# Attention beside an MLP on one core: the attention loop by two query blocks, with one stretch of 64x64 tiles for both

## Chip, cores and metric

One core of a Trainium2 chip. The metric is the device time of one execution in microseconds, lower is better.

## The reference

```python
xn = layernorm(x)                                   # x: 2048 x 640
q, k, v = split(xn @ wqkv)                          # 32 heads of 20 columns
scores = (q @ k.T) * 20 ** -0.5
mask = (i - j >= 0) & (i - j < 256)                 # each query sees 256 keys at most
s = softmax(where(mask, scores, -1e9)) @ v          # then @ wo
h = relu(xn @ w1 + b1) ** 2                         # 640 -> 1536
g = silu(h @ w2 + b2)                               # 1536 -> 640
return x + (s @ wo) * g
```

Everything is float32. The kernel splits each float32 operand of a product into two float16 parts, high and low, and adds three products (high by high, high by low, low by high).

## The kernel before

Three parts follow one another. The first normalizes x, turns it, and makes the values and the first 128 query and key columns. The second is the attention loop. The third multiplies the attention's output with `wo` and joins both branches.

The attention loop has 16 head pairs `p` of 16 query blocks `q` of 128 rows, so 256 steps `s`, and 13 more in which the later stages of the last blocks finish. All engines' orders are written out by hand: each engine does its instructions in the order in which the code gives them. In a step, in this order:

- `scores` (L547): for both heads, two half blocks of 64 queries against 320 keys, four products in tiles of 64x64 of the array (L557). `maxima` (L560): VectorE adds the mask and takes the largest score of each row (L568), one instruction a head. Every fourth step `max_rows` (L577) turns the maxima of four blocks on TensorE; they are written by DMA as two more rows of the queries.
- `scores_t` (L596), ten steps behind (`LAG`): the scores once more with keys as rows, the maxima being subtracted by the two more rows, again four 64x64 products (L604). `exps` (L607): ScalarE's exponential of both heads, 768 columns, into `p32` (L609), and two selects on GpSimd that cut the mask's triangles (L610, L612).
- `low` (L620), two steps behind that: VectorE's float16 rest `pl` of the exponentials (L623).
- A part of the filler (`EARLY_FILL`), then `flush`, which empties finished filler groups; then `high` (L615), one step behind `exps`: ScalarE's float16 copy `ph` (L617). Then the rest of the filler.
- `values` (L626), for two blocks in every second step: products of `ph` and `pl` with the values (L637), 24 for two blocks. Every fourth block `normed` (L641) copies the sums (L644), and VectorE and GpSimd divide.

The filler (`filler`, L804) is a generator of all other products, so that TensorE has work in each step: 32 groups of 15 products of 512 columns for the other query and key columns (`qkps`), then for 8 blocks of 256 rows 12 groups of 15 products of 256 columns (`hps`, the hidden layer) and 4 groups of 36 products of 320 columns (`yps`), and at the end the output product (`wops`, from L922). `fill` (L995) takes from it as much as the step's share `per`. When a group is finished, its evacuation is put on a list: for `qkps` a ScalarE copy and a VectorE rest (L80, L81); for `hps` ScalarE's relu and square (L855, L856), VectorE's square (L858) and a subtraction on GpSimd (L859); for `yps` one VectorE instruction (L886). `tick` (L739) splits one waiting piece of weights into its parts, ScalarE first, then VectorE (L125, L126), or squares it (L775).

The eight PSUM banks of 2 KiB (512 float32 columns) a partition are dealt out in pools: three for filler groups (`pmm`), two for scores (`pat`), two for turned scores (`pst`, one tile `sts[0]`, L594), one for the values' sums (`po_`).

Of the kernel before, what the change touches and what calls it, by code (L numbers as in the profile page):

```python
# [14 lines left out]
P = 128  # L15
# [19 lines left out]
LAG = 10  # L35
PB = 6
# [3 lines left out]
EARLY_FILL = 0.35  # L40
SWING = 0.3
# [16 lines left out]
def attn_mlp_kernel(ctx: ExitStack, tc, x, wqkv, wo, w1, b1, w2, b2, out):  # L58
# [4 lines left out]
    pmm = ctx.enter_context(tc.tile_pool(name="pmm", bufs=3, space=PSUM))  # L63
    pat = ctx.enter_context(tc.tile_pool(name="pat", bufs=2, space=PSUM))
    pst = ctx.enter_context(tc.tile_pool(name="pst", bufs=1, space=PSUM))
    po_ = ctx.enter_context(tc.tile_pool(name="po", bufs=1, space=PSUM))
# [148 lines left out]
    with tc.tile_pool(name="ph1v", bufs=4) as p1v, tc.tile_pool(name="ph1", bufs=2) as p1, tc.tile_pool(name="ph1x", bufs=4) as p1b, tc.tile_pool(name="ph1w", bufs=1) as p1w:  # L215
        xts, xns, mvs, rstds, turns, vts = {}, {}, {}, {}, {}, {}
        wv = [p1w.tile([P, KC, D], F16, name=f"wv{p}") for p in range(2)]
        sums = po_.tile([P, 64], F32, tag="o", name="sums")
# [312 lines left out]

    at1 = ctx.enter_context(tc.tile_pool(name="at1", bufs=1))
# [12 lines left out]
    mts = {}  # L545

    def scores(p, q, between):  # L547
        i = p % 2
        r = [pat.tile([P, 4 * P], F32, tag="s", name="sps") for h in range(2)]
        rows = between and between(r[0])  # L550
        nk = min(WIN + HB, (q + 1) * P)
        for j in range(2):
            q0 = q * P + j * HB
            k0 = max(0, q0 - WIN)
            for h, ps in enumerate(r):
                rows_ = slice(HB * h, HB * h + HR)
                nc.tensor.matmul(ps[HB * j:HB * (j + 1), :nk], qs[i][rows_, q0:q0 + HB], ks[i][rows_, k0:k0 + nk], start=True, stop=True)  # L557
        return (r, mask if q > 1 else mask0[:, 2 * P - nk:], nk), rows

    def maxima(p, q, r):  # L560
        if q % 4 == 0:
            mts[p, q // 4] = mtp_.tile([P, 8], F32, tag="mt", name="mt")
        mt = mts[p, q // 4]
        r, mk, nk = r
        for h, ps in enumerate(r):
            junk = mtp_.tile([P, WIN + HB], BF16, tag="junk", name="junk")
            at_ = 4 * h + q % 4
            nc.vector.tensor_tensor_reduce(out=junk[:, :nk], in0=ps[:, :nk], in1=mk, scale=1.0 / MAX_UNIT, scalar=-3.0e38, op0=ALU.add, op1=ALU.max, accum_out=mt[:, at_:at_ + 1])  # L568
        if q % 4 == 3:
            mp = mps[q // 4 % 2]  # L570
# [6 lines left out]
    def max_rows(p, g, tp=None):  # L577
        i = p % 2
        mp = mts.pop((p, g))
        if tp is None:  # L580
            tp = pat.tile([P, 4 * P], F32, tag="s", name="mtp")
        tp = tp[:, 3 * P:3 * P + P // 2].bitcast(F16)
# [9 lines left out]
    pts = {}  # L592
    ots = {}
    sts = []  # L594

    def scores_t(p, kb):  # L596
        i = p % 2
        n = min(3, NT - kb) * P
        ps = sts[0]
        for j in range(2):  # L600
            c0, c1 = HB * j, min(n, WIN + HB * (j + 1))
            for hh in range(2):
                rows_ = slice(HB * hh, HB * hh + ER)
                nc.tensor.matmul(ps[HB * j:HB * (j + 1), hh, c0:c1], ks[i][rows_, kb * P + HB * j:kb * P + HB * (j + 1)], qs[i][rows_, kb * P + c0:kb * P + c1], start=True, stop=True)  # L604
        return ps, n

    def exps(p, kb, ps, n):  # L607
        p32 = at2.tile([P, 2, 3 * P], F32, tag="p32", bufs=3, name="p32")
        nc.scalar.activation(p32[:, :, :n], ps[:, :, :n], AF.Exp, scale=esc[0], bias=ebias)  # L609
        nc.gpsimd.affine_select(p32[:, :, 0:P], p32[:, :, 0:P], pattern=[[0, 2], [1, P]], compare_op=ALU.is_ge, fill=0.0, base=0, channel_multiplier=-1)  # L610
        if n == 3 * P:
            nc.gpsimd.affine_select(p32[:, :, 2 * P:], p32[:, :, 2 * P:], pattern=[[0, 2], [-1, P]], compare_op=ALU.is_gt, fill=0.0, base=0, channel_multiplier=1)  # L612
        return p32

    def high(p, kb, p32, n):  # L615
        ph = at4.tile([P, 2, 3 * P], F16, tag="ph", name="ph")
        nc.scalar.activation(ph[:, :, :n], p32[:, :, :n], AF.Copy)  # L617
        phs[p, kb] = (ph, p32, n)

    def low(p, kb):  # L620
        ph, p32, n = phs.pop((p, kb))
        pl = at4.tile([P, 2, 3 * P], F16, tag="pl", bufs=PB - 1, name="pl")
        nc.vector.tensor_sub(pl[:, :, :n], p32[:, :, :n], ph[:, :, :n])  # L623
        pts[p, kb] = (ph, pl)

    def values(p, q):  # L626
        if q % 4 == 0:
            ots[p, q // 4] = po_.tile([P, 4, 2, VW], F32, tag="o", name="ops")
        ot = ots[p, q // 4]
        vp = vps[p]  # L630
        ksr = list(range(max(0, q - 2), q + 1))
        for hh in range(2):
            m = 0
            for k in ksr:
                for t in pts[p, k]:
                    m += 1
                    nc.tensor.matmul(ot[:, q % 4, hh, :], t[:, hh, (q - k) * P:(q - k + 1) * P], vp[:, k // 4, k % 4, hh, :], start=m == 1, stop=m == 2 * len(ksr))  # L637
        if q >= 2:
            del pts[p, q - 2]

    def normed(p, g):  # L641
        ot = ots.pop((p, g))
        osb = at2.tile([P, 8, VW], F32, tag="osb", name="osb")
        nc.scalar.activation(osb, ot.rearrange("p a h w -> p (a h) w"), AF.Copy)  # L644

        def rest():
            rs = at2.tile([P, 8], F32, tag="rs", name="rs")
            nc.vector.reciprocal(rs, osb[:, :, VW - 1])
            on = at2.tile([P, 8, DH], F32, tag="on", name="on")
            nc.gpsimd.tensor_add(on, osb[:, :, 0:DH], osb[:, :, DH:2 * DH])  # L650

            def last():
                nc.gpsimd.tensor_mul(on, on, rs.unsqueeze(2).to_broadcast([P, 8, DH]))
                post(o_d[g].rearrange("t p d -> p t d")[:, :, 2 * DH * p:2 * DH * (p + 1)], on.rearrange("p (t h) d -> p t (h d)", t=4))
            norm.append(last)
        return rest


    early = at2.tile([P, 1], F32, tag="early", bufs=1, name="early")
    state = [0.0, 0.0, 0]  # L660
# [10 lines left out]
    pending, late = [], []  # L671
# [5 lines left out]
    def flush(upto=None):  # L677
        for f in late[:]:
            f()
        late.clear()  # L680
        while pending and (upto is None or flushed[0] < upto):
            flushed[0] += 1
            pending.pop(0)()

# [32 lines left out]
    AGE = 2  # L717
# [65 lines left out]
    def second_scales():  # L783
        s2, i2 = weight_scale("w2", totals("w2_t", pmm.tile([P, NF], F32, tag="mm", name="sums2"), mlp["g2"]))
        so, io = weight_scale("wo", totals("wo_t", pmm.tile([P, KC], F32, tag="mm", name="sumso"), sso))
# [18 lines left out]
    def filler():  # L804
        ws = {1: {w: tuple(qkw[0][:, 1, i, j] for j in range(2)) for i, w in enumerate("qk")}}
        for g in range(1, KC):
            ensure(f"g{g}")
            for b in range(NB):
# [17 lines left out]
                for w in "qk":  # L826
                    hi, lo = ws[g][w]
                    ps = pmm.tile([P, BT], F32, tag="mm", name="qkps")
# [271 lines left out]
```

## Time and profile before

| | us |
|---|---|
| median of three runs | 849.09 (848.74 to 850.21) |
| profiled execution | 848.83 |
| its span | 847.0 |
| before the attention loop | 118.7 |
| attention loop | 648.8 |
| output product and end | 79.5 |

The span is the time from the first to the last instruction in the trace. An engine's busy time is the union of its instructions' times. Consecutive instructions of one engine overlap a little, so what an instruction costs its engine is read from its start to the next one's start, where nothing is waited for.

### The profile page before, as it was taken

The page shows a single profiled execution, that of the slowest core. Times are in us where ns is not written, and L with a number is a line of the kernel's source. Part 1 is how long each engine was busy: PE and PEld are TensorE (multiplying, and loading weights), DVE is VectorE, ACT ScalarE, POOL GpSimd, SP SyncE. Part 2 cuts the span into 40 slices and gives each one's busy share as a digit, 9 for nine tenths or more (in the row PEclk, how much of TensorE's full clock was granted, in tenths as well). Part 3 has the DMA queues.
Part 4 walks back from the last instruction along what each step waited for, and adds up shares of the span by engine and source line. Part 5 has one row for each costly group of instructions (what it writes and reads, how often), then busy time and mean ns, then how long its engine had stood idle before and what let it go on. Part 6 is the DMA issues. An engine that isn't in the chain of part 4 may idle for free.

```text
span 847.0 us, 25061 instructions
## 1 busy us (share of the span) xinstructions
PE 822.7 (97%) x9426; PEld 553.4 (65%) x9426; DVE 692.8 (82%) x1897; ACT 648.1 (77%) x1028; POOL 485.0 (57%) x874
## 2 busy tenths in 40 slices
PE   8999998999999999999999999999999999999998
PEld 7765553444444676776766766766767767767775
DVE  6776566788999998898988998888988888975655
ACT  5565446998898997897997997987987988993321
POOL 2000001456665798796896986886986977961000
PEclk9999999999999999999999999999999999999999
DMA  7994349755475311213111222113122113055883
GB/s 245 250 349 129 135 127 283 234 162 157 127 229 163 111 44 55 66 33 89 51 49 50 65 52 65 50 33 84 30 76 65 49 42 99 11 180 171 301 297 126
DMA packets 100498, 104.52 MB, mean 123 GB/s; under 512 B 42520, under 2 KB 72856, under 8 KB 100376
## 3 DMA queue, kind: packets, MB, share of 16 engines
q1 hardware_dynamic: 100376, 102.91, 39.8%
q8 instruction: 74, 1.21, 0.6%
q14 instruction: 48, 0.39, 0.2%
HBM read 65.67 MB, written 36.83 MB: 121 GB/s over the span
## 4 chain that ended last, share of the span: by engine, by line
PE 60%; ACT 14%; POOL 8%; DVE 7%; issue 6%; DMA 3%; SPq 1%; DVEq 0%; ACTq 0%; POOLq 0%
PE yps L882 17%; PE wops L688 8%; PE vps L292 7%; PE hps L688 6%; ACT p L609 5%; PE ops L637 5%; PE qkps L688 5%; PE sps L557 4%; ACT ph L617 3%; PE qkps L503 3%; DVE junk L568 3%; PE stps L604 2%; POOL hh L859 2%; DVE pl L623 2%; ACT relu L855 2%
## 5 line engine op out<-in xcount | busy, mean ns | idle before, releaser
L609 ACT ACTIVATE p<-stps,ebias,esc 128x768 f32<-128x768 f32 (+2 forms) x256 | 242.1, 946 | 59.7 <-PE stps L604 48.9
L568 DVE CUSTOM_DVE_ANT_0 junk<-sps,mask 128x320 bf16<-128x320 f32 (+2 forms) x512 | 220.8, 468 | 49.0 <-PE sps L557 41.4
L623 DVE TENSOR_TENSOR pl<-p,ph 128x768 f16<-128x768 f32 (+2 forms) x256 | 248.8, 972 | 3.8 <-ACT ph L617 3.2
L610 POOL TENSOR_SCALAR_AFFINE_SELECT p<-p 128x256 f32<-128x256 f32 x256 | 163.8, 640 | 86.0 <-ACT p L609 76.7
L617 ACT ACTIVATE ph<-p 128x768 f16<-128x768 f32 (+2 forms) x256 | 203.1, 793 | 2.4 <-POOL p L612 1.6
L688 PE MATMUL hps<-xT,w 128*128 128x256 f16 x1440 | 176.2, 273 | 0.0
L882 PE MATMUL yps<-w,hh 128*128 128x320 f16 x1152 | 174.6, 300 | 0.0
L688 PEld LDWEIGHTS <-w 128*128 128x128 f16 x1440 | 132.6, 98 | 36.0 <-issue 17.2
L882 PEld LDWEIGHTS <-hh 128*128 128x128 f16 x1152 | 104.7, 98 | 57.0 <-issue 18.1
L688 PE MATMUL qkps<-xT,qkw 128*128 128x512 f16 x480 | 115.4, 380 | 0.5 <-DVE w_t L153 0.5
L612 POOL TENSOR_SCALAR_AFFINE_SELECT p<-p 128x256 f32<-128x256 f32 x224 | 103.6, 463 | 0.0
L557 PE MATMUL sps<-ks,qs 60*64 60x320 f16 (+2 forms) x1024 | 87.4, 312 | 6.8 <-DVE mt L568 5.9
L637 PE MATMUL ops<-vp,ph 128*128 128x41 f16 x1440 | 89.8, 181 | 0.0
L637 PE MATMUL ops<-vp,pl 128*128 128x41 f16 x1440 | 89.5, 180 | 0.0
L637 PEld LDWEIGHTS <-ph 128*128 128x128 f16 x1440 | 84.5, 96 | 6.2 <-issue 0.6
L604 PE MATMUL stps<-qs,ks 62*64 62x320 f16 (+4 forms) x1024 | 80.9, 293 | 6.7 <-ACT p L609 6.1
L573 POOL CAST mp<-mt 128x8 f16<-128x8 f32 x64 | 44.6, 698 | 70.0 <-DVE mt L568 69.7
L637 PEld LDWEIGHTS <-pl 128*128 128x128 f16 x1440 | 78.9, 96 | 5.6
L859 POOL TENSOR_TENSOR hh<-sq,hh 128x256 f16<-128x256 f32 x96 | 74.9, 782 | 6.4 <-DVE sq L858 4.3
L688 PEld LDWEIGHTS <-qkw 128*128 128x128 f16 x480 | 41.6, 98 | 55.4 <-issue 11.7
L292 PE MATMUL vps<-wv,xT 128*128 128x320 f16 x480 | 70.3, 303 | 3.2 <-ACT xT L261 1.6
L557 PEld LDWEIGHTS <-qs 60*64 60x64 f16 x1024 | 32.5, 103 | 55.2 <-issue 47.4
(150 smaller groups left out, 1032.4 us busy)
## 6 DMA issues: line engine op xcount, KB each, us to landing
ks<-k_d SPq DMA_DIRECT2D x64, 120.0 KB
qs<-q_d SPq DMA_DIRECT2D x64, 120.0 KB
raw<-in_B_w_dram SPq DMA_DIRECT2D x24, 320.0 KB
v_d<-vt SPq DMA_DIRECT2D x8, 656.0 KB
vp<-v_d SPq DMA_DIRECT2D x16, 328.0 KB
xt<-in_A_x_dram SPq DMA_DIRECT2D x16, 320.0 KB
k_d<-shm SPq DMA_DIRECT2D x20, 256.0 KB
q_d<-shm SPq DMA_DIRECT2D x20, 256.0 KB
```

What stands on the lines that cost most here:

```text
L292: nc.tensor.matmul(ps, xT[b][:, xp, c, t * P:(t + 1) * P], wv[wp][:, c, nh * HALF:(nh + 1) * HALF], start=n == 0, stop=n == 3 * KC - 1)
L557: nc.tensor.matmul(ps[HB * j:HB * (j + 1), :nk], qs[i][rows_, q0:q0 + HB], ks[i][rows_, k0:k0 + nk], start=True, stop=True)
L568: nc.vector.tensor_tensor_reduce(out=junk[:, :nk], in0=ps[:, :nk], in1=mk, scale=1.0 / MAX_UNIT, scalar=-3.0e38, op0=ALU.add, op1=ALU.max, ...
L604: nc.tensor.matmul(ps[HB * j:HB * (j + 1), hh, c0:c1], ks[i][rows_, kb * P + HB * j:kb * P + HB * (j + 1)], qs[i][rows_, kb * P + c0:kb * ...
L609: nc.scalar.activation(p32[:, :, :n], ps[:, :, :n], AF.Exp, scale=esc[0], bias=ebias)
L610: nc.gpsimd.affine_select(p32[:, :, 0:P], p32[:, :, 0:P], pattern=[[0, 2], [1, P]], compare_op=ALU.is_ge, fill=0.0, base=0, channel_multip ...
L612: nc.gpsimd.affine_select(p32[:, :, 2 * P:], p32[:, :, 2 * P:], pattern=[[0, 2], [-1, P]], compare_op=ALU.is_gt, fill=0.0, base=0, channel ...
L617: nc.scalar.activation(ph[:, :, :n], p32[:, :, :n], AF.Copy)
L623: nc.vector.tensor_sub(pl[:, :, :n], p32[:, :, :n], ph[:, :, :n])
L637: nc.tensor.matmul(ot[:, q % 4, hh, :], t[:, hh, (q - k) * P:(q - k + 1) * P], vp[:, k // 4, k % 4, hh, :], start=m == 1, stop=m == 2 * le ...
L688: nc.tensor.matmul(ps, a, b_, start=j == 0, stop=j == n - 1)
L882: nc.tensor.matmul(pss[nh], hs[fc][:, hp, tt * P:(tt + 1) * P], lin1(w2t, (2 * fc + wp) * D + nh * HALF, HALF), start=fc == 0 and j == 0, ...
```

## The change

The loop goes by periods `t` of two query blocks: 128 periods and 8 more (`OUT`). A period has this order:

1. `flush`, which empties all finished filler groups; on every second period the turning of the maxima.
2. `values` for two blocks, eight periods behind, into that one of two accumulators `accs` that the filler isn't using, and `taken`, ScalarE's copy of the sums, every period.
3. `low` for two blocks (1536 columns in one instruction), two periods behind `scores_t`.
4. `scores_t` for two blocks, five periods behind (`LAG`), then `scores` for two blocks: one stretch of 64x64 products. Each head has a tile of three banks, `pairs[h]`: scores of the two blocks in columns 0 to 320 and 320 to 640, the turned maxima from 640, the turned scores from 768 to 1536. A product that would cross a bank's edge is cut in two there (`cuts`).
5. `exps` of head 0, the maxima of head 1 for both blocks, `exps` of head 1, the maxima of head 0. The selects take all four blocks at once.
6. Filler in four parts of 0.3, 0.3, 0.25 and the rest, with `flush`, stores and loads between them. After the first part `high`, one period behind `exps`, in one instruction of 1536 columns.

A filler group asks for its bank when it begins (`bank`): the accumulator that was not last used, or, late in a period and if it is short, the first bank of a score tile. A group isn't begun if less than `GUARD` of the period's share is left; the rest is made up in the next period. In the last part of the kernel the groups go round all eight banks.

The sort that did the last three hidden groups' products last in the first half block's `yps` groups is gone. The PSUM pools of the first part are closed at its end.

```diff
-LAG = 10
-PB = 6
+LAG = 5
+OUT = LAG + 3
+PB = 4
+GUARD = 0.7
+LATE = 2.2
+BANK = 512
...
+    psum = ctx.enter_context(tc.tile_pool(name="psum", bufs=1, space=PSUM))
+    pairs = [psum.tile([P, 3 * BANK], F32, name=f"pair{h}") for h in range(2)]
+    accs = [psum.tile([P, BANK], F32, name=f"acc{i}") for i in range(2)]
...
+    SCORE_AT = (0, WIN + HB)
+    TURNED_AT = 2 * (WIN + HB)
+    TSCORE_AT = 3 * BANK - 6 * P
+
+    def cuts(o, n):
+        x = [o] + [y for y in range(BANK, 3 * BANK, BANK) if o < y < o + n] + [o + n]
+        return list(zip(x, x[1:]))
...
+    def bank(cost, n=BANK):
...
+        if state[0] > state[4] + LATE and cost < state[3] - state[0] - GUARD and used != {2, 3}:
+            key = 2 + len(used)
+            used.add(key)
+        else:
+            last[0] = key = 1 - last[0]
+        flush(owner.get(key, 0))
+        return key, (accs + pairs)[key][:, 0:n]
...
+            if e:
+                ot = accs[1 - last[0]][:, 0:4 * VW].rearrange("p (q h w) -> p q h w", q=2, h=2)
+                values(*e, ot)
+                norm = taken(*e, ot)
+            if c:
+                low(c)
             if b:
-                stp = scores_t(*b)
-            if a:
-                maxima(*a, sc)
...
+                scores_t(*b)
+                p32s[b] = at2.tile([P, 3 * BANK], F32, tag="p32", bufs=3, name="p32")
+            if a:
+                scores(*a)
+            for h in range(2):
+                if b:
+                    exps(b[1], p32s[b], h)
+                if a:
+                    for q in range(2):
+                        maxima(a[0], 2 * a[1] + q, 1 - h)
...
+            fill(0.3 * per)
+            between()
+            tick()
+            d = at(t - LAG - 1)
             if d:
-                low(*d)
...
+                high(d, p32s.pop(d))
+            fill(0.3 * per)
+            between()
+            fill(0.25 * per)
+            between()
             tick()
-            if c:
-                high(*c, *exs.pop(c))
...
+            fill(state[3] - state[1])
```

`between` is `flush`, the stores that are due, and loads.

More of the change, by code (lines that the diff above doesn't have):

```diff
@@ L545, in attn_mlp_kernel @@
     mts = {}
-    def scores(p, q, between):
-        i = p % 2
[L549 to L558, printed above, removed]
@@ L615, in high @@
[L615 to L639, printed above, removed]
@@ L1005, in attn_mlp_kernel, with at, between @@
     with tc.manual_schedule(engines={E_.PE, E_.Activation, E_.DVE, E_.Pool, E_.SP}):
[L1006 to L1012 removed]
+        p32s, loads = {}, []
+        def at(n):
+            return divmod(n, NT // 2) if 0 <= n < count else None
+        def between():
+            flush()
             post_all()
             issue(RATE)
[L1015 removed]
+        for t in range(periods):
+            state[2] = t
+            post_all()
+            issue(RATE)
+            a, b, c, e = (at(t - lag) for lag in (0, LAG, LAG + 2, OUT))
@@ L1034, in attn_mlp_kernel @@
-            rows = between = None
-            if s % 4 == 1 and 1 < s <= NP * NT + 1:
-                def between(tp=None, s=s):
-                    return max_rows((s - 2) // NT, (s - 2) % NT // 4, tp)
-            if a:
-                sc, rows = scores(p, q, between)
-            elif between:
-                rows = between()
+            flush()
+            used.clear()
+            rows = max_rows((t - 2) // (NT // 2), (t - 2) % (NT // 2) // 2) if t % 2 == 0 and 2 <= t <= count else None
```

279 lines of the change are left out of this document (152 added, 127 removed).

## The prediction

> **What bounds the kernel now.** I read the page's busy shares first, then the stretches of the trace in which the filler is of one kind, then single rows of three engines. The shares are TensorE (PE), VectorE (DVE), ScalarE (ACT) and GpSimd (POOL):
>
> ```profile
> span 847.0 us, 25061 instructions
> PE 822.7 (97%) x9426; PEld 553.4 (65%) x9426; DVE 692.8 (82%) x1897; ACT 648.1 (77%) x1028; POOL 485.0 (57%) x874
> 118.70:281.00 162.30, 155.12 (x1573) 73.22 (x1573) 138.40 (x409) 133.71 (x206) 82.54 (x169) 1.00 0.63 191
> 404.00:434.40 30.40, 30.36 (x445) 23.63 (x444) 28.36 (x79) 29.10 (x50) 27.75 (x46) 1.00 0.18 49
> 495.50:525.80 30.30, 30.30 (x410) 20.14 (x408) 25.44 (x79) 24.82 (x34) 22.65 (x42) 1.00 0.24 68
> 767.50:847.00 79.50, 74.83 (x585) 56.37 (x583) 47.01 (x90) 21.85 (x34) 0.99 (x2) 1.00 0.68 233
> ```
>
> The last four lines are stretches: length, then busy us of PE, PEld, DVE, ACT, POOL, the granted clock (1.00 everywhere) and DMA. The loop over query blocks runs from 118.7 to 767.5, 648.8 us for 269 steps, so two steps (one period of the changed loop) take 4.82 us. The first stretch has qk filler, the second hps, the third yps. PE is the bound on average, but beside hps filler ACT is busy 29.10 of 30.40 us and DVE 28.36: there three engines are full at once. After 767.5 there is only the output product.
>
> What PE pays for a stretch of 64x64 tiles, in the rows of PE (start, us, line, form, count):
>
> ```profile
> 504.03 0.33 PE L557 MATMUL sps<-ks,qs 60*64 60x320 f16 x4
> 504.19 0.31 PE L604 MATMUL stps<-qs,ks 62*64 62x320 f16 x4
> 504.43 1.40 PE L882 MATMUL yps<-w,hh 128*128 128x320 f16 x9
> 505.66 0.18 PE L637 MATMUL ops<-vp,ph 128*128 128x41 f16 x1
> ...
> 508.46 0.25 PE L557 MATMUL sps<-ks,qs 60*64 60x128 f16 x4
> 508.54 0.31 PE L604 MATMUL stps<-qs,ks 62*64 62x320 f16 x4
> ```
>
> Four tiles go as one group: 0.16 us for 320 columns (504.03 to 504.19), 0.08 for 128 (508.46 to 508.54). A line through the two is 0.027 us and 0.00042 a column. From the last group to the first yps it is 0.24, so 0.08 more than the group itself. A yps takes 0.137 (nine from 504.43 to 505.66).
>
> **The change, part by part.** I cost PE first, then the order of the other engines.
>
> *One stretch for two blocks.* One way out of the tile mode (0.08 us) goes in each of 128 periods. The way in isn't free of other work in these rows; taken like the way out it makes 0.16 a pair, 20 us in all (at least 10, if the way in costs nothing; at most 26, at 0.2). *Cuts at bank edges:* the second block's scores (columns 320 to 640) become 192 and 128, the first turned block (768 to 1152) becomes 256 and 128. By the line above these are 0.107+0.080 and 0.134+0.080 instead of 0.16 each: 0.08 a period, 10 us (at least 3.5, if only one extra start of 0.027 counts). Net on PE: 20-10, about -10 us, with ends +0 and -22. *Half as many calls:* `high` and `low` handle 1536 columns at once, the two selects four blocks, and the output copy is taken every period. These save or cost about 0.1 us a period on engines beside PE; they enter below by their rows.
>
> *PSUM.* The filler has two accumulators instead of three, and the values take the one that it isn't using. The rule for borrowing a score bank asks that over 2.2 of the 3.125 us of filler be done and that the group be shorter than the rest less 0.7, so under 0.225; the shortest product group is 1.67. It is never used for one inside the loop.
>
> *A new wait.* Each head has one tile of three banks of 512 columns. The second block's scores end at column 640, the turned scores start at 768: both lie in the second bank. ACT's exp reads one, DVE's maxima the other. If two readers of a bank are kept apart, the code's order decides: exp of head 0 beside the maxima of head 1, then exp of head 1 **after** the maxima of head 1. In the kernel before, no bank has two readers that don't already wait for one another by their data, so no row shows this. The nearest row is that exp waits for DVE where they share a tile of SBUF:
>
> ```profile
> ACT p L609 <- PE stps L604: 48.9, 74, 1.8
> ACT p L609 <- DVE pl L623: 7.6, 12, 1.4
> PE stps L604 <- ACT p L609: 6.1, 17, 1.1
> PE sps L557 <- DVE mt L568: 5.9, 7, 1.6
> ```
>
> The columns are total us, times, longest. The last two are what PE waits for the readers now, 12 us at most to be gained. Below zero the new wait can't go; at zero it leaves the PE sum. What it costs at most follows from what stands in front of the maxima on DVE. I take the wait as real: the heads are crossed in the code for that, and an order between users of one tile is what the second row shows.
>
> *The chain that this closes.* DVE's order in a period is `low`, the maxima of head 1 (two), of head 0 (two), then what the filler needs. `low` needs `high` of the period before. `high` stands behind both exps on ACT. So exp of head 1 -> `high` -> `low` of the next period -> two maxima -> exp of head 1: a period can't be shorter than that. The rows:
>
> ```profile
> 407.86 0.99 ACT L609 ACTIVATE p<-stps,ebias,esc 128x768 f32<-128x768 f32 x1 [0.58 <-DVE ysb L886]
> 408.75 0.56 ACT L855 ACTIVATE relu<-hps,m,m 128x256 f32<-128x256 f32 x1
> 409.34 0.42 ACT L856 ACTIVATE hh<-relu 128x256 f16<-128x256 f32 x1
> 409.66 0.83 ACT L617 ACTIVATE ph<-p 128x768 f16<-128x768 f32 x1
> 410.39 0.98 ACT L609 ACTIVATE p<-stps,ebias,esc 128x768 f32<-128x768 f32 x1
> 416.90 0.61 ACT L617 ACTIVATE ph<-p 128x512 f16<-128x512 f32 x1
> 417.42 0.97 ACT L609 ACTIVATE p<-stps,ebias,esc 128x768 f32<-128x768 f32 x1
> ...
> 408.18 0.47 DVE L568 CUSTOM_DVE_ANT_0 junk<-sps,mask 128x320 bf16<-128x320 f32 x1
> 408.59 0.94 DVE L623 TENSOR_TENSOR pl<-p,ph 128x768 f16<-128x768 f32 x1
> 409.46 0.41 DVE L858 TENSOR_TENSOR sq<-relu 128x256 f32<-128x256 f32 x1
> 413.27 1.25 DVE L623 TENSOR_TENSOR pl<-p,ph 128x768 f16<-128x768 f32 x1
> 414.44 0.62 DVE L858 TENSOR_TENSOR sq<-relu 128x256 f32<-128x256 f32 x1
> 418.47 0.68 DVE L623 TENSOR_TENSOR pl<-p,ph 128x512 f16<-128x512 f32 x1
> 419.07 0.68 DVE L858 TENSOR_TENSOR sq<-relu 128x256 f32<-128x256 f32 x1
> ```
>
> Start to start, exp takes 0.89 (407.86 to 408.75). `high` takes 0.73 for 768 columns (409.66 to 410.39) and 0.52 for 512, so 0.21 for 256 more: 1.36 for 1536, and its end is 0.10 later (0.83 against 0.73). `low` takes 0.87 (408.59 to 409.46) and 0.60 for 512, so 1.68 for 1536. A maximum takes 0.41 to the next and 0.47 to its end. From one engine's end to the next's start I take 0.03, the gap after relu's end (408.75+0.56 to 409.34). Sum: 0.89+1.46+0.03+1.68+0.41+0.47+0.03 = 4.97 us. The last two key blocks of a head pair are narrower by half (768 columns for 1536): about 0.1 less on exp, 0.5 on `high`, 0.7 on `low`, and its first maxima are shorter by 0.3: 1.6 in 8 periods, mean 4.77. With it closed on 121 of the 136 periods (it starts at the seventh and ends when the scores do): 577 us. The first 7 and last 8 have less work; by filler (3.1) and a part of the stretch and values I take 25 and 31 us. So far 633, less than 648.8: alone the chain is no loss.
>
> *What stands in the chain.* The code fixes where each filler group is emptied: before `high` (first flush of the period) or behind it. Walking through it, of 96 hps groups 31 come before `high` and 65 behind. Before: relu and square, 409.66-408.75 = 0.91 on ACT, all in the chain. Behind: relu runs after `high`, DVE's sq waits for it, and `low` of the next period waits behind sq. That is 0.56+0.03+0.41, less the 0.13 from `high`'s own end: 0.87. Sum 28+57 = 85 us. For qk groups:
>
> ```profile
> 206.03 0.59 ACT L80 ACTIVATE shm<-qkps 128x512 f16<-128x512 f32 x1
> 206.50 0.84 ACT L617 ACTIVATE ph<-p 128x768 f16<-128x768 f32 x1
> 206.69 0.69 DVE L81 SCALAR_TENSOR_TENSOR shm<-qkps,shm 128x512 f16<-128x512 f32 x1
> ...
> 211.46 0.83 ACT L125 ACTIVATE qkw<-raw,g_s 128x640 f16<-128x640 f32 x1
> 212.18 0.84 ACT L617 ACTIVATE ph<-p 128x768 f16<-128x768 f32 x1
> ```
>
> After the seventh period 9 come before `high` (0.47 each) and 17 behind (0.59+0.03+0.69-0.13 = 1.18): 4+20 = 24 us. The 35 weight pieces (0.72 on ACT each) sit before `high` or after it in turn; 25 of them in the chain make 18 (0 to 50). yps groups are emptied by DVE alone, in the time in which it waits for `high`: nothing. If that cover went, 32 evacuations of a maximum's length (0.47), 15 us.
>
> **The sum.** 633+85+24+18 = 760 us against 648.8: +111. PE's ten us don't count, since its work of some 4.65 us a period (4.82 less 10 us of saving and 12 of waits over 128 periods) fits under the chain. Behind 767.5 the tail keeps its 79.5; eight banks there instead of the present set may give 1. The profiled execution took 848.83 us for its 847.0 span, 0.3 under the median of 849.09. Prediction: 848.8+111 = **960 us**. The ends of this case: 915 if half the emptying terms hide (-64) while `low` is dearer (1.17 for 768 columns from 413.27 to 414.44; half of that excess is 0.15 a period, +18), and 995 if all pieces are in the chain (+32).
>
> The Trainium skill speaks against this change here: "PSUM — Partial Sum Buffer", section "PSUM bank collisions raise a hardware error", says that two engines on one bank and quadrant at once raise an error, two readers included, and that the compiler puts a dependency between them. No run here shows it yet. By it the time is 960; without it, the first rival's 833.
>
> **The rivals.** *No wait between the readers (other side).* ACT and DVE run free, PE stays the bound, and gets its -10 and about 6 of the 12 us of waits: 849-16 = **833** (820 to 845). It decides if exp of head 1 starts at exp of head 0's end while `low` still runs. For it: PE's 97%, and no row of such a wait. Against: both lie in one bank. *The chain holds but the emptying hides.* Its plain 4.77 with half or less of the 127 us of terms: 633+30 to 633+64, and the 200 us outside the loop, so **863 to 897**. For it: DVE idles in yps stretches (25.44 of 30.30). Against: in the hps stretch nothing is idle that could hide it. *Nothing measurable, 849:* no wait between readers, but ACT sets the hps stretches. Its 29.10 us there don't shrink, and two accumulators behind `high` make PE wait what the stretch saves: 51 periods of 0.2 against -10.
>
> **Chances.** The chain as summed 0.70 (its own range 915 to 995); chain with hidden emptying 0.12; no wait 0.13; nothing 0.05. A difference of 0.2% (1.7 us) is about what this kernel's runs can tell. Slower: 0.70+0.12, less 0.02 for the lower edge of the second; faster: 0.13 and a little of the last, 0.14; same 0.06. The range takes the first two cases and the last: 848 to 995, which leaves out the 833 and a tail above, under 0.2.
>
> **What would show it.** In the changed profile: exp waiting for the maxima's line on DVE, around 100 times, in sum over 80 us; `low` of some 1.7 us waiting for `high`; hps stretches near 41 us instead of 30.4 and yps ones near 30; PE's share under 90%; four maxima in a row behind `low`. In PE's rows, one stretch in a period with groups of 0.13, 0.08, 0.16, 0.16, 0.11, 0.08. I am wrong if exp of head 1 follows that of head 0 by 0.9 us in most periods, or if hps stretches stay at 30.

## The result, and the profile after

The changed kernel takes 1032.01 us (1026.98 to 1033.41, four runs), the kernel before 848.91 beside it: ratio 1.214, 95% interval 1.210 to 1.219. It is 183 us slower; 960 was predicted. One of the two executions of the variant exps_first below took 2006 us at full granted clock, for a reason that isn't known, and is left out. The profiled execution of the changed kernel took 1031.83 us. The page's span, busy shares and chain:

```profile
span 1030.1 us, 26382 instructions
PE 841.4 (82%) x10386; PEld 595.8 (58%) x10386; DVE 673.3 (65%) x1786; ACT 665.6 (65%) x1012; POOL 438.9 (43%) x634
ACT 33%; PE 25%; DVE 20%; issue 19%; DMA 2%; SPq 0%; ACTq 0%; POOL 0%; DVEq 0%
```

PE's share fell from 97% to 82%, and no engine took its place: ACT and DVE are less busy than before too. So waits between engines are the first suspect. From the list of waits, without GpSimd's and the weight loads' (us in total, times, longest):

```profile
ACT p L623 <- DVE mt L576: 121.1, 104, 2.8
DVE sq L900 <- ACT relu L897: 104.3, 86, 2.3
DVE pl L645 <- ACT ph L638: 55.1, 47, 1.8
PE acc L658 <- ACT relu L897: 45.3, 45, 2.0
PE acc L658 <- DVE shm L79: 25.7, 17, 3.5
PE acc L728 <- ACT relu L897: 25.5, 21, 3.1
```

The first is the predicted wait: exp (L623) waits for the maxima (L576). In the timeline of the two engines beside hps filler it stands with its whole chain, ACT first, then DVE (start, us; in brackets the idle time before):

```profile
571.68 0.99 ACT L623 ACTIVATE p<-pair,ebias,esc 128x768 f32<-128x768 f32 x1 [1.69 <-DVE mt L576]
572.57 1.47 ACT L638 ACTIVATE ph<-p 128x1536 f16<-128x1536 f32 x1
573.94 0.56 ACT L897 ACTIVATE relu<-acc,m,m 128x256 f32<-128x256 f32 x1
574.85 0.55 ACT L897 ACTIVATE relu<-acc,m,m 128x256 f32<-128x256 f32 x1
576.03 0.99 ACT L623 ACTIVATE p<-pair,ebias,esc 128x768 f32<-128x768 f32 x1
578.71 0.99 ACT L623 ACTIVATE p<-pair,ebias,esc 128x768 f32<-128x768 f32 x1 [1.69 <-DVE mt L576]
...
575.50 0.62 DVE L900 TENSOR_TENSOR sq<-relu 128x256 f32<-128x256 f32 x1 [0.48 <-ACT relu L897]
576.05 1.75 DVE L645 TENSOR_TENSOR pl<-p,ph 128x1536 f16<-128x1536 f32 x1
577.72 0.48 DVE L576 CUSTOM_DVE_ANT_0 junk<-pair,mask 128x320 bf16<-128x320 f32 x1
578.13 0.48 DVE L576 CUSTOM_DVE_ANT_0 junk<-pair,mask 128x320 bf16<-128x320 f32 x1
```

Exp of head 1 at 571.68, `high`, two relus, DVE's sq behind the second, `low`, two maxima, exp of head 1 at 578.71: 7.03 us, with no idle time over 0.1 us between a step and the next (ACT's squares behind the relus are left out of the rows). Beside yps filler, where only the bare chain is left, the same exp starts at:

```profile
608.53 0.99 ACT L623 ACTIVATE p<-pair,ebias,esc 128x768 f32<-128x768 f32 x1 [1.21 <-DVE mt L576]
613.61 0.99 ACT L623 ACTIVATE p<-pair,ebias,esc 128x768 f32<-128x768 f32 x1 [1.62 <-DVE mt L576]
```

That is 5.08 us for a period (predicted 4.97). The stages of qk filler, of one block's hps filler, of one block's yps filler, and the tail, by windows (length, busy us of PE, PEld, DVE, ACT, POOL, granted clock, DMA):

```profile
121.00:327.00 206.00, 160.28 (x1818) 83.86 (x1814) 139.07 (x383) 135.85 (x200) 60.98 (x115) 0.93 0.48 149
480.70:521.80 41.10, 30.56 (x455) 25.36 (x455) 27.38 (x74) 31.40 (x50) 26.38 (x34) 0.96 0.14 38
596.30:628.00 31.70, 28.30 (x422) 20.79 (x421) 22.97 (x66) 22.60 (x28) 20.85 (x26) 1.00 0.20 58
923.00:1030.00 107.00, 82.60 (x553) 56.36 (x550) 46.42 (x88) 22.04 (x32) 0.00 (x0) 0.93 0.49 176
```

Measured from the first qk product to the first output product, the loop takes 801.9 us (before 650.6: +151), what is ahead of it 121.2 (118.9: +2), and the tail behind it 107.1 (77.6: +30). So two places lost the time, the loop and the tail.

### The profile page after: what moved, and what is told of

It reads as the page before. It is cut to its first block, busy times and chain, and to the rows that moved or that the text cites. A ratio compares the mean times of both kernels' runs of the same rounds, so it can differ in the third digit from the quotient of the medians.

```text
span 1030.1 us, 26382 instructions
## 1 busy us (share of the span) xinstructions
PE 841.4 (82%) x10386; PEld 595.8 (58%) x10386; DVE 673.3 (65%) x1786; ACT 665.6 (65%) x1012; POOL 438.9 (43%) x634
## 4 chain that ended last, share of the span: by engine, by line
ACT 33%; PE 25%; DVE 20%; issue 19%; DMA 2%; SPq 0%; ACTq 0%; POOL 0%; DVEq 0%
ACT ph L638 14%; DVE pl L645 10%; ACT p L623 8%; PE acc L728 6%; PE vps L290 6%; PE pair L728 5%; DVE junk L576 5%; ACT relu L897 4%; PE qkps L501 3%; PE acc L658 2%; ACT hh L898 2%; DMA raw<-in_B_w_dram 1%; ACT shm L78 1%; DVE mt L576 1%; PE pair L615 1%
## 5 line engine op out<-in xcount | busy, mean ns | idle before, releaser
L623 ACT ACTIVATE p<-pair,ebias,esc 128x768 f32<-128x768 f32 (+2 forms) x288 | 250.4, 884 | 155.1 <-DVE mt L576 121.1
L645 DVE TENSOR_TENSOR pl<-p,ph 128x1536 f16<-128x1536 f32 x144 | 221.1, 1544 | 56.5 <-ACT ph L638 55.1
L576 DVE CUSTOM_DVE_ANT_0 junk<-pair,mask 128x320 bf16<-128x320 f32 (+2 forms) x512 | 213.1, 467 | 15.7 <-PE pair L565 9.2
L728 PE MATMUL acc<-xT,w 128*128 128x256 f16 x1440 | 180.2, 282 | 36.6 <-ACT relu L897 23.1
L638 ACT ACTIVATE ph<-p 128x1536 f16<-128x1536 f32 x144 | 179.7, 1259 | 0.0
L728 PE MATMUL acc<-w,hh 128*128 128x320 f16 x1152 | 170.4, 304 | 5.0 <-ACT osb L667 2.4
L658 PE MATMUL acc<-vp,ph 128*128 128x41 f16 x1440 | 91.0, 182 | 76.9 <-ACT relu L897 45.3
L627 POOL TENSOR_SCALAR_AFFINE_SELECT p<-p 128x512 f32<-128x512 f32 x128 | 81.8, 639 | 144.1 <-ACT p L623 141.8
L728 PE MATMUL acc<-xT,qkw 128*128 128x512 f16 x480 | 118.9, 402 | 5.0 <-ACT osb L667 5.0
L658 PE MATMUL acc<-vp,pl 128*128 128x41 f16 x1440 | 90.9, 182 | 0.0
L629 POOL TENSOR_SCALAR_AFFINE_SELECT p<-p 128x512 f32<-128x512 f32 x112 | 79.7, 711 | 0.0
```

What stands on the lines that cost most here:

```text
L576: nc.vector.tensor_tensor_reduce(out=junk[:, :nk], in0=pairs[h][:, o:o + nk], in1=mk, scale=1.0 / MAX_UNIT, scalar=-3.0e38, op0=ALU.add, o ...
L623: nc.scalar.activation(dst, src, AF.Exp, scale=esc[0], bias=ebias)
L627: nc.gpsimd.affine_select(r[:, :, 0:P], r[:, :, 0:P], pattern=[[0, 4], [1, P]], compare_op=ALU.is_ge, fill=0.0, base=0, channel_multiplier=-1)
L629: nc.gpsimd.affine_select(r[:, :, 2 * P:], r[:, :, 2 * P:], pattern=[[0, 4], [-1, P]], compare_op=ALU.is_gt, fill=0.0, base=0, channel_mul ...
L638: nc.scalar.activation(h_, s_, AF.Copy)
L645: nc.vector.tensor_sub(l_, s_, h_)
```

## The experiments

The main theory is that the chain through exp, `high`, `low` and the maxima holds the loop (A), and that the tail's 30 us are waits between users of one tile (D). Its rivals for what is left are the turning of the maxima (E), the two accumulators, whose emptying stands behind `high` (F), and other passes through DVE's queue (G, H). In the recorded expectations the letters shift: the accumulators are B in the first ones and F from ef_tail4_turn2 on; E is the clock or the order of the evacuations in tail4; F means several chains of nearly one length in low_twice, and the turning in ef_tail4_turn. All edits are against the changed kernel. "Loop" and "tail" are measured as above, in the profiled run.

| run | us | loop | tail | ratio to before (95%) |
|---|---|---|---|---|
| changed kernel | 1032.0 | 801.9 | 107.1 | 1.214 (1.210 to 1.219) |
| low_twice | 1260.6 | 1030.6 | 107.2 | 1.484 (1.480 to 1.488) |
| low_late | 997.8 | 764.1 | 107.5 | 1.174 (1.166 to 1.182) |
| exps_first | 971.2 | 740.6 | 107.4 | one run beside 849.8 |
| high_early | 1032.0 | 800.3 | 107.9 | 1.214 (1.211 to 1.218) |
| max_bank0 | 1028.0 | 798.0 | 107.1 | 1.210 (1.207 to 1.214) |
| tail4 | 1000.5 | 800.0 | 77.0 | 1.177 (1.174 to 1.181) |
| turn_odd | 1034.7 | 804.5 | 107.1 | 1.218 (1.215 to 1.222) |
| ef_tail4_turn | 933.3 | 734.2 | 77.0 | 1.099 (1.096 to 1.102) |
| ef_tail4_turn2 | 924.7 | 726.0 | 76.9 | 1.089 (1.087 to 1.091) |
| ef_tail4_turn2_hm | 919.1 | 717.5 | 77.0 | 1.083 (1.081 to 1.086) |
| all_ll_hm | 1039.7 | 840.9 | 76.9 | 1.223 (1.220 to 1.226) |
| all_ll_hl | 1038.7 | 837.6 | 76.9 | 1.223 (1.222 to 1.225) |
| all_ll_hl_flip | 1038.6 | 840.6 | 77.0 | 1.223 (1.221 to 1.225) |
| all_ll_hm_out1 | 1020.2 | 822.6 | 77.0 | 1.198 (1.194 to 1.201) |
| all_ll_hl_out1 | 1014.3 | 815.6 | 77.0 | 1.192 (1.190 to 1.195) |
| all_ll_hl_out1_flip | 1013.7 | 815.9 | 77.0 | 1.193 (1.188 to 1.198) |
| low_mid | 990.7 | 759.6 | 107.1 | 1.168 (1.165 to 1.171) |
| low_mid_all | 944.5 | 744.5 | 77.0 | 1.113 (1.111 to 1.114) |

**Is the chain what holds the loop?** `low` issued twice; `low` moved behind the maxima; both exps ahead of all maxima:

```diff
 # low_twice
             nc.vector.tensor_sub(l_, s_, h_)
+            nc.vector.tensor_sub(l_, s_, h_)
 # low_late: low(c) goes from ahead of scores_t to behind rows() and norm()
 # exps_first
                 if b:
                     exps(b[1], p32s[b], h)
+            for h in range(2):
                 if a:
                     for q in range(2):
-                        maxima(a[0], 2 * a[1] + q, 1 - h)
+                        maxima(a[0], 2 * a[1] + q, h)
```

> The changed kernel with every `low` done twice on VectorE (the second writes the same numbers again), 1.68 us more in each of some 121 periods; VectorE is busy only 65% of the changed kernel's span. Theory A (low lies on the chain that sets the period): the whole of it shows, 121 x 1.68 = 203 us, 1215 to 1240 in all. Theory F (several chains are nearly as long, the turning of the maxima among them, so that cutting one at low gained only 34 us): the sum is the same in this direction, since the longest chain still grows; 1200 or more. Rival (VectorE's idle time takes it): 1045 or less.

> The changed kernel, but VectorE does `low` after the four maxima instead of before them. Theory A (the chain exp of head 1 -> high -> low -> two maxima -> exp of head 1 sets the period): low leaves the chain. What is left beside hps filler is relu -> square on VectorE -> two maxima -> exp -> (relu, square) -> high -> relu, 0.41+0.03+0.89+0.03+0.89+0.91+1.36+0.56 = 5.1 us instead of 7.0; yps and qk periods fall to TensorE's 4.65 to 4.8. hps stages 33 to 35 us each instead of 41.5, yps 29.5 instead of 30.8, qk stage 165 to 178 instead of 206; in all 890 to 925 us. Rival B (two accumulators for the filler, emptied behind high, are what holds TensorE): nothing of that is touched, 1000 us or more.

> The changed kernel, but ScalarE's exponentials of both heads come first in the code and the maxima of both heads after them, so that VectorE waits for ScalarE in the bank they share and never the other way. Theory A: the chain is cut at its other link. ScalarE's own 5.0 us a period bound the hps stages (33 to 35 us), TensorE the others; 890 to 930 us, and ScalarE's wait for the maxima (121 us in the changed kernel) is gone, while VectorE waits for the exponentials. Rival B (accumulators): 1000 us or more. Rival C (it is low's place on VectorE alone that costs, not the order of the two readers): 1000 or more here, and a gain only with low behind the maxima.

The second `low` adds 228.6 us; the 1260.6 are 21 above the 1215 to 1240 of theory A. The second one is dearer than the 1.68 us that were assumed:

```profile
801.02 2.11 DVE L646 TENSOR_TENSOR pl<-p,ph 128x1536 f16<-128x1536 f32 x1
803.05 0.28 DVE L576 CUSTOM_DVE_ANT_0 junk<-pair,mask 128x128 bf16<-128x128 f32 x1
```

That is 2.03 us from its start to the next one's; the median of all whole ones is 1.89, and all of them, the narrow ones too, are about 230 us. So nearly the whole addition went into the time, though DVE was busy only 65%: in nearly every period `low` lies on what sets the time. Moving `low` away does away with the wait. Of its 121.1 us the list of low_late has 4.8 left:

```profile
PE pair L593 <- POOL mp L586: 49.8, 53, 1.7
ACT p L623 <- DVE mt L576: 4.8, 14, 0.8
```

But the time falls by 34 us only, and in exps_first (no such wait in the list at all) by 61. Both miss what A asked for (890 to 925 and 890 to 930), and low_late's 998 nearly meets the 1000 of rival B, the accumulators. So A is the first limit of the changed kernel, and close behind it stands another. The longest of PE's waits in low_late is now for the turned maxima (L593) that GpSimd prepares; the runs with a later turning, below, show that this wait isn't the next limit by itself.

**Bank or tile?** From the third block of a pair on, the maxima read columns 0 to 320 only, all in bank 0 (the second block's maxima are taken over the first one's scores, and the exponent's bias is changed); exp reads columns 768 to 1536, banks 1 and 2.

```diff
-in0=pairs[h][:, o:o + nk]
+in0=pairs[h][:, (o if q < 2 else 0):(o if q < 2 else 0) + nk]
```

> The changed kernel, but the maxima of a pair's later blocks are taken from the first block's scores for both blocks, so VectorE reads columns 0 to 320 (the first bank of a head's tile) and never the bank that the exponential reads. The second block's maxima are left out that way, and the exponential's bias is lowered to keep numbers finite. If the wait between the two readers goes by bank, exp of head 1 no longer waits for VectorE in seven of eight periods, and it comes to 960 to 985 us, as with the exponentials first. If it goes by tile (three banks), as the output product's waits seem to, nothing changes: 1025 to 1035, and ScalarE's wait for the maxima stays above 100 us.

```profile
ACT p L623 <- DVE mt L576: 122.1, 104, 2.8
```

And two exps of head 1 in ACT's timeline:

```profile
570.30 0.99 ACT L623 ACTIVATE p<-pair,ebias,esc 128x768 f32<-128x768 f32 x1 [1.68 <-DVE mt L576]
577.33 0.99 ACT L623 ACTIVATE p<-pair,ebias,esc 128x768 f32<-128x768 f32 x1 [1.69 <-DVE mt L576]
```

The time stays in the range said for an order by tile (1025 to 1035): 104 waits as before, exp to exp 7.03 us again. From the third block on the readers have no bank in common, and still wait: in this kernel the order is kept by tile, not by bank.

**The tail.** In the changed kernel the tail takes eight banks in turn, six of them in the two three-bank tiles. The timeline of the changed kernel shows what that does:

```profile
927.78 0.55 DVE L1011 SCALAR_TENSOR_TENSOR res<-pair,o_inv,yb 128x320 f32<-128x320 f32 x1 [3.09 <-issue]
928.39 0.66 PE L971 MATMUL pair<-ident,ob 128*128 128x128 f32 x4 [0.70 <-DVE res L1011]
929.09 0.55 DVE L1011 SCALAR_TENSOR_TENSOR res<-pair,o_inv,yb 128x320 f32<-128x320 f32 x1 [0.22 <-PE pair L971]
929.69 0.66 PE L971 MATMUL pair<-ident,ob 128*128 128x128 f32 x4 [0.65 <-DVE res L1011]
```

PE starts at 928.39 when DVE ends reading another group's result, DVE's next read starts when PE's group ends, and so on: they take turns on a tile whose banks are different. The test uses four banks, each the first of its own tile:

```diff
-            last[0] = (last[0] + 1) % 8
-            key = last[0]
+            last[0] = (last[0] + 1) % 4
+            key = (0, 2, 1, 3)[last[0]]
...
-            return key, accs[key][:, 0:n] if key < 2 else pairs[k % 2][...]
+            return key, (accs + pairs)[key][:, 0:n]
```

> The changed kernel, but after the loop the filler goes round four banks, each in a tile of its own (the two accumulators and the first bank of each head's tile), instead of eight banks, six of which lie in the two three-bank tiles. Theory D (in the output product TensorE waits for VectorE and ScalarE reading other banks of the same tile, since the wait goes by tile): the part after the loop falls from 108 us to 80 to 88, in all 1005 to 1012 us, with half as many banks. Rival E (the tail is slow since the granted clock fell to half in it, or by the order of its evacuations): 105 us or more there, no change of the total beyond 5 us.

With half the banks the tail falls from 107.1 to 77.0 us, more than D asked for and nearly to the 77.6 of the kernel before. PE's listed waits in it fall from 20.5 to 1.4 us, and its granted clock rises from 0.93 to 1.00; what the clock alone is worth wasn't separated, but the edit changes only which banks the tail uses. D is shown: eight banks in four tiles work worse than four banks in four tiles.

**`high` ahead of the exps**, to take it out of the chain:

```diff
+            if d:
+                high(d, p32s.pop(d))
             for h in range(2):
                 if b:
                     exps(b[1], p32s[b], h)
```

> The changed kernel, but ScalarE does `high` before the two exponentials of its period instead of after the first part of the filler. Theory A: high then runs while TensorE does its stretch, low of the next period finds it done, and the chain is exp -> what empties the filler -> square on VectorE -> low -> two maxima -> exp: 0.89+0.91+0.56+0.03+0.41+1.68+0.89+0.03 = 5.4 us beside hps (35 us a stage), nothing of it beside yps (29 us); qk stage about 175; in all 900 to 935 us. Rival B (accumulators emptied too late): it gains as well, since the filler's evacuation no longer stands behind high; B alone would put it below the run with low behind the maxima by 30 us or more.

A miss for A and B: no gain. By the list of waits, `high`, which copies what GpSimd's selects leave, waits for them ahead of the exps, with the exps behind it on ACT, and DVE behind the exps; no run tests this reading:

```profile
DVE junk L576 <- ACT p L623: 109.2, 74, 3.0
ACT ph L638 <- POOL p L629: 56.3, 35, 2.8
ACT p L623 <- DVE mt L576: 24.8, 37, 1.9
```

**The turning one period later**, alone and with the two edits that gained; then also ahead of the period's `flush` (turn2), so that DVE's copy of the turned row (L597) isn't behind a square that waits for ACT; then `high` behind the second part of the filler (hm):

```diff
-            rows = max_rows((t - 2) // ...) if t % 2 == 0 and 2 <= t <= count else None
+            if t % 2 == 1 and 3 <= t <= count + 1:
+                max_rows((t - 3) // (NT // 2), (t - 3) % (NT // 2) // 2)()
+                post_all()
```

> The changed kernel, but the maxima are turned one period later, and the rows are copied and sent off at once at the period's start. TensorE stood up to 4 us before the turning, at the head of its period, until GpSimd had the maxima ready. With the chain A still closed this is only partly in the way: 1005 to 1028 us. If the turning itself were what sets the period: 980 or less.

> Three edits together: both exponentials first (971 alone), the tail's four tiles (-31 alone), the turning one period later. Theory F (behind chain A the next limit is TensorE's wait for the turned maxima at the head of every second period): periods beside yps fall from 4.8 to 4.65-4.75 and beside hps to ScalarE's 5.0-5.3, qk stage to 175, the granted clock back over 0.985; 865 to 905 us. If the two edits only add up and the turning doesn't matter: 935 to 945.

> Both exps ahead of the maxima, the tail round four tiles, and the turning one period later and now ahead of the emptying at the period's start, so that VectorE's copy of the turned row no longer stands behind a `sq` that waits for ACT's relu. Measured against 933.3 us of the same kernel with the copy behind that emptying. Theory E (the copy of the turned row, late in VectorE's queue, holds PE's next stretch of the tile `pair0` in every second period: 18 waits of 1.3 us listed, 23.4 us, and what follows from them): 885 to 912 us. Theory F (what is left comes from only two accumulators, which PE finds unemptied behind ACT's `high`): 925 to 937 us.

> As the run before, and ACT's `high` is issued behind the second stretch of filler and its emptying instead of behind the first. Theory F (the emptying behind `high` holds PE's values: 44 us of listed waits for relu and shm): 15 to 35 us less than the run before. Theory E: within 6 us of the run before. A third outcome, 10 us or more above it, would say that `high` so late holds `low` and with it the maxima of the next period.

Alone the turning gives nothing (1034.7, where 1005 to 1028 was expected), as chain A still holds the loop. With the chain and the tail mended it is worth little: 971 less the tail's 31 would be 940, 933 was measured (865 to 905 was expected if the turning were the next limit); its better place gives 9 us, where E asked for 21 to 48, and the place of `high` 5.5, where F asked for 15 to 35. E and F are both too large.

**`low` late in the best version** (low_late's edit on top; then `high` behind the third part of the filler, hl; then the filler's next group in the other accumulator than the values, flip):

```diff
+                if held_:
+                    last[0] = 1 - last[0]
                 values(*e, ot)
```

> Both exps ahead of the maxima, tail round four tiles, turning a period later and ahead of the emptying, `high` behind the second stretch of filler, and now also `low` behind the maxima. Measured against 919.1 us of the same kernel with `low` ahead of them. Theory G (in what is left, VectorE's `low` ahead of the maxima still holds PE's next stretch): 880 to 905 us. Theory F (PE finds its two accumulators unemptied: ACT's part of the emptying stands behind the exps and `high`): 912 to 925 us, as `low` is no part of that.

> As the run before, with `high` behind the third stretch of filler and its emptying, so that ACT empties accumulators ahead of it in nearly every period. Theory F: 15 to 35 us less than the run before, most of it in the qk stage, where values wait 1.2 to 1.5 us a period for an emptying that stood behind `high`. Theory G: within 6 us of it.

> As the run before, and where no filler group is open when the values start, the next group takes the other accumulator than the values (before: the same one, so that it waits for ACT's `osb`). Theory F: a further 5 to 25 us less (19 waits of 15.8 us are listed for `osb`, 0.5 to 0.7 us each in the hps stages). Theory G: within 5 us of the run before.

The first misses G and F by over 110 us, and the other two stay within 1.2 us of it: another limit holds all three. The timeline of all_ll_hl has it:

```profile
590.76 1.87 ACT L623 ACTIVATE p<-pair,ebias,esc 128x768 f32<-128x768 f32 x2 [0.38 <-PE pair L565]
591.78 0.49 DVE L576 CUSTOM_DVE_ANT_0 junk<-pair,mask 128x320 bf16<-128x320 f32 x1 [1.19 <-ACT p L623]
593.50 2.06 DVE L645 TENSOR_TENSOR pl<-p,ph 128x1536 f16<-128x1536 f32 x1
595.61 0.19 PE L658 MATMUL acc<-vp,pl 128*128 128x41 f16 x1 [1.34 <-DVE pl L645]
596.19 0.47 PE L615 MATMUL pair<-qs,ks 62*64 62x256 f16 x12
596.99 1.87 ACT L623 ACTIVATE p<-pair,ebias,esc 128x768 f32<-128x768 f32 x2 [0.38 <-PE pair L565]
```

Exps at 590.76, maxima from the end of the first, `low` at 593.50, the values at its end, the stretch, exps at 596.99: 6.23 us. The same `low` that was too early ahead of the maxima is too late behind them. So the values were put one period later (`OUT = LAG + 4`, a fifth `ph` buffer):

> As all_ll_hm (1039.7 us), with the values one period later (OUT = LAG + 4, one more buffer of `ph`). Theory H (with `low` behind the maxima a chain closes through one period: exps, four maxima, `low`, values, stretch, exps, of 6.2 us): it is opened, as the values then take a `low` that ended a period before: 860 to 895 us, below the 919.1 us with `low` ahead of the maxima, because PE's next stretch no longer waits for `low`. Theory F (unemptied accumulators alone): 912 to 925 us. If the values' `low` is not what closes it: 1030 to 1040 us.

> As all_ll_hl (1038.7 us), with the values one period later; against the run before it differs in the place of `high` alone (behind the third stretch of filler instead of the second). Theory F: 10 to 30 us less than the run before. Theory H: within 6 us of the run before.

> As the run before, and where no filler group is open at the values, the next group takes the other accumulator than the values. Theory F: 5 to 25 us less than the run before (a wait of 0.5 to 0.7 us for `osb` in each hps period goes). Theory H: within 5 us of it.

That opens the chain, but for 20 to 25 us, where H asked for 145 or more. The list of all_ll_hl_out1:

```profile
DVE junk L576 <- ACT p L623: 226.3, 135, 6.5
PE pair L615 <- DVE mrow L597: 59.8, 42, 4.8
```

DVE still idles 226 us for the exps (256 in all_ll_hl), and its later work (`low`, squares, the turned row's copy) ends so late that PE's next stretch waits 59.8 us, where it waited 16.1 in all_ll_hl. That this is what holds the loop now is read from the list, not tested. `high` one place later gives 6 us here, the flip nothing.

**`low` between the two heads' maxima**, in the changed kernel's order of exps, alone, and with tail4, turn2 and hm:

```diff
             for h in range(2):
...
                         maxima(a[0], 2 * a[1] + q, 1 - h)
+                if c and h == 0:
+                    low(c)
```

> One edit against the changed kernel: VectorE's `low` is issued between head 1's maxima and head 0's instead of ahead of both. Theory H (what holds each of the variants is one pass through VectorE's queue: whatever of its 1.75 us `low`, four maxima and the copy stands between an exp and the next exp on the shared tiles): exp 1 then waits only for two maxima that end 0.9 us behind the stretch, while exp 0 still runs, and the values take a `low` of the period before that ended early; no chain is left, the list shows no ACT wait for the maxima, and the time is 915 to 955 us, of which some 30 are the tail. Theory F (two accumulators, 70 us of the loop left in the best variant so far, 919 with the tail mended): 945 to 975 us. If neither, as with `low` behind all maxima: about 998 us.

> The run before with the three other edits at once: the tail round four tiles, the turning a period later and ahead of the emptying, `high` behind the second stretch of filler; against the kernel of 919.1 us it differs in the order of exps, maxima and `low` alone. Theory H: 845 to 890 us. Theory F: 905 to 925 us. Without an effect of the order: 919 us.

Both miss, H by 36 and 55 us, F by 16 and 20. Alone the edit gains 41 us (low_late: 34). With the rest it is 25 us worse than ef_tail4_turn2_hm, from which it differs in the order of exps, maxima and `low` only. The list of low_mid_all:

```profile
DVE junk L576 <- PE pair L565: 96.3, 82, 4.9
PE pair L593 <- DVE mt L576: 18.7, 27, 2.5
```

DVE waits 96.3 us for the stretch (3.1 in ef_tail4_turn2_hm), and PE's turning waits 18.7 us for maxima that end late (1.0 there). ACT hardly waits for the maxima any more (6.6 us), as H said, but its "no chain is left" doesn't follow from that; which pass sets the time here wasn't worked out.

**What stays open.** The best version, ef_tail4_turn2_hm, is still 8.3% slower than the kernel before; its loop is 67 us longer. PE's own waits in it are these:

```profile
PE pair L615 <- DVE mrow L597: 22.6, 17, 2.8
PE acc L727 <- ACT osb L667: 15.8, 19, 2.9
PE acc L658 <- DVE shm L79: 15.6, 15, 2.5
PE acc L658 <- ACT relu L896: 11.3, 12, 1.3
PE acc L727 <- ACT relu L896: 8.2, 16, 0.7
PE acc L658 <- DVE ysb L918: 7.7, 14, 2.5
```

59 us on the two accumulators and 23 on the tile of head 0, against 12 on PSUM before. The excess of 70 is of the loss's size, but that is arithmetic on a list: the runs aimed at the accumulators changed their order, not their number, and moved at most 5.9 us. A third accumulator was not tried, as the eight banks are given out.

## Why the prediction was right or wrong

- *The new wait: right.* About 100 times and over 80 us were said; 104 times and 121.1 us came. max_bank0 shows that in this kernel banks aren't the criterion, since 122.1 us of it stay, with no bank in common in seven of eight periods. The Trainium skill ("PSUM — Partial Sum Buffer", section "PSUM bank collisions raise a hardware error") says that the compiler adds a dependency between engines on the same bank and quadrant. The trace agrees that the readers wait (121.1 us); the wait that is left in max_bank0 doesn't come from a rule by bank.
- *The chain: right in kind and nearly in size.* 4.97 predicted, 5.08 measured beside yps; 41 for the hps stages and 42.9 measured, 30 for the yps stages and 31.6 (means of eight, from the first product of one kind to the first of the next). low_twice shows that what is added to `low` lengthens the loop nearly in full. The 833 us of the free readers and the 863 to 897 of hidden emptying are out: DVE's sq stands between relu and `low` in the rows above.
- *The step that failed: "Behind 767.5 the tail keeps its 79.5; eight banks there instead of the present set may give 1."* From the first output product it is 107.1 for 77.6, +30. The prediction saw the three-bank tiles, and costed their wait only for exp and the maxima; tail4 shows that it is the same wait once more, between PE and DVE.
- *The loop's sum: mis-sized as well, +111 for +151.* This is the larger part of the 72 us between 960 and 1032. By the prediction's terms the qk stage takes 193 us (25 for the start, 26.5 periods of 4.77, 24 and 18), the eight hps stages 329 in all and the eight yps stages, with the shorter end, 236; measured are 206, 343 and 253. A part of it is the bare chain: beside yps most periods are 5.07 us long, and the eight of a head pair, each at its most frequent length, make 39.3, so 4.91 a period for 4.77. Over 121 periods that is 17 us. Where the rest comes from is open.
- *Costed at nothing: the turning of the maxima.* As long as the chain holds that was right (turn_odd: no gain). Without it PE waits 50 us for it (low_late), but turning later then gained only some 7 us (ef_tail4_turn).
- *"Alone the chain is no loss": half right.* The chain and its terms are only the first limit. Taking it away gives 34 to 61 us of the 151; other limits lie close behind, among them passes through DVE's queue, and the prediction, which counted PE's 4.65 us as the next limit, had none of them.
- *PE's gain from fewer stretches: there in the rows, not in the time.*

```profile
609.85 0.47 PE L615 MATMUL pair<-qs,ks 62*64 62x256 f16 x12
...
610.52 3.30 PE L728 MATMUL acc<-w,hh 128*128 128x320 f16 x23
```

From the stretch's first product to the next filler it is 0.67 us for two blocks; before, it was 0.40 for each (504.03 to 504.43). That is 0.13 a period, 17 us in all, where a gain of 10 between 0 and 22 was forecast. PE's idle time covers it in every version.

## What to carry to other kernels

Put what different engines read at the same time into tiles of their own, not only into banks of their own: in these runs the order was kept by tile, and four banks in four tiles served the tail 30 us better than eight in four. When a loop runs on several hand-ordered queues, look for each pass that leads through them back to its start, before and after every move; here moving one instruction could open one pass and close another (7.03 us in the changed kernel, 6.23 in all_ll_hl). Compare the sum along each pass with the period, not with each engine's share of busy time.

## What was not expected of the hardware

PE's granted clock fell where PE idled: the windows of the changed kernel above show 0.93 in the qk stage, 0.96 in an hps stage and 1.00 in a yps stage, where before it was 1.00 in all of them. The trace's clock records have 21 spells at half rate after the first 60 us, 82 us in sum, each 3.41 us or longer (before: one, in the last 0.4 us of the span); in low_twice 67 spells, 301 us. In the 3.41 us ahead of each of the 21, PE was busy for 0 to 2.03 us, by median 1.36, and only one of these windows was wholly idle. The Trainium skill ("TensorE: Matmul & The Clock Gate", Part 1) says that the clock is halved after an idle window of some 3.4 us. The trace agrees on the length; but as the profile counts busy time, PE need not be idle for the whole of such a window. What these spells cost by themselves was not separated, as the queues' waits set the loop's length.
